# Block-sparse attention and a feed-forward layer on one core: the first pair's operands built by engines, other early transfers and conversions re-ordered

## The chip, the core and the metric

The kernel runs on one core of one Trainium2 chip. The metric is the device time of one execution in microseconds; the time before is the median of three runs, 979.95 us (977.11 to 985.35). PE is the matmul engine, DVE, ACT and POOL are the vector, scalar and GpSimd engines, SP is the engine that issues most transfers.

## What is computed

The reference, cut to what matters:

```python
def _attn_ref(q, k, v, sampled_blocks):            # 4 x 8 heads, S = 768, D = 64, blocks of 32
    scores = np.matmul(q, k.transpose(0, 1, 3, 2)) / np.sqrt(D)
    mask = np.abs(blk_i - blk_j) <= 1              # neighbours, first and last block, sampled blocks
    ...
    scores = np.where(mask, scores, -1000000000.0)
    attn = np.exp(scores - np.max(scores, axis=-1, keepdims=True))
    attn = attn / (np.sum(attn, axis=-1, keepdims=True) + 1e-09)
    return np.matmul(attn, v)

def _moe_ref(x, w_in, w_out):                      # 3072 tokens, 512 -> 2048 -> 512
    h = x @ w_in
    return (h - np.tanh(h)) @ w_out
```

The weights arrive as double precision words; the kernel reads them as pairs of 32-bit words and puts the bits of a single precision number together.

## The kernel before

Thirty-two heads are worked as 16 pairs, then the feed-forward layer follows (`FFN`, units of 512 tokens by 128 hidden columns, 24 + 24 matmuls of 512 columns each). Products are made exact enough by splitting an operand into a high part, which the matmul holds exactly, and a low part, the rest.

A **slot** (`slots`, three of them) holds a pair's operands in four areas: `sA` and `sB` hold the high parts of k and q in partitions 0 to 63, in 64 to 87 the mask by blocks of keys and the one-hot code of the query's block, and in 88 a row of ones and the row of negated maxima; `sC` and `sD` hold the parts for the two cross products. For each pair, `load` fetches k, q and v (SP); `prep_qk` transposes k and q on PE (L198), ACT copies out the high part (`hik`, `hiq`, L200), DVE subtracts for the low part (`lok`, `loq`, L201); `dist` sends 64 partitions at a time into the slot, twelve transfers a pair on SP (L213). `fill` (L185) sends the one-hot code and the mask into each slot, and `setup` makes the mask on DVE (L163 to L178) from two small loads. POOL writes ones to 25 partitions of each slot (L177) and makes the identity.

For each head, `smax` (L255, tiles `sm`) multiplies the high parts for the six query tiles and DVE takes each row's maximum (L259); `smax_fin` transposes the six columns (L264), negates them (`nm`, L266) and sends them to the slot (L267). `qk_exp` (L283, L284, tiles `st`) then forms the full scores with the maximum in, and ACT takes the exponential (`pe`, L287). `split` makes a half precision high and low part (`ph` on ACT or DVE, `pl` on POOL or DVE, L295 to L299), `accum` multiplies them with v (L313 to L322), `norm` divides (L331 to L335), `spill` stores to memory (L341). `prep_v` scales v by its largest magnitude, which starts with a reduction on DVE (`am`, L221).

PSUM holds three `big` tiles (for `sm`, `st`, `pt` and others) and two `one` tiles (for `av`, `pmt`, `pa`).

The first six blocks of weights (`NPRE`) are converted in the attention stage: `load_pre` fetches one (512 KB), `convert_pre` has DVE do three operations of 128 x 512 (L436, L439, L442) and stores the result, and `fetch_w` and `split_w` bring it into a freed slot at the end of attention. Two further blocks are fetched to `stage` by `stage_w`. In the feed-forward stage the same three operations keep their intermediate words in a PSUM tile (`self.cv`).

The order of the work comes from a table of times: each step is put down with `at(time, ...)` in units of one score tile (six to a head, twelve to a pair; head h's maxima run from 6h + TSM on, its exponentials from 6h on), the steps are sorted and called in that order, and a scheduler that simulates the engines then settles each engine's order. Dependencies without a wait (`add_manual_dep` with NoSync) tell it that one instruction shall stand behind another. `urgent` and `after` use them to put later transfers behind the first pair's.

Of the kernel before, what the change touches and what calls it, by code (L numbers as in the profile page):

```python
# [106 lines left out]
def attention(ctx, tc, q, k, v, samp, w_in, w_out, blocks, xscr, ident, ps, slots, wt, f2, ffn):  # L107
# [33 lines left out]
    def load(pr, which="kqv", first=None):  # L141
        r = loads.setdefault(pr, [])
        for nm, src in ((n, x) for n, x in (("k", k), ("q", q), ("v", v)) if n in which):
            t = p2.tile([P, S], F32, tag="raw" + nm, name=f"raw{nm}{pr}", bufs=2)
            d = nc.sync.dma_start(out=t, in_=src[pr])
# [4 lines left out]
    load(0, "kq")  # L150

    def setup():
        for i in range(NV):
# [4 lines left out]
        nc.sync.dma_start(out=sp_i[R, :], in_=samp)
# [4 lines left out]
        nc.vector.tensor_copy(out=sp_f[R, :], in_=sp_i[R, :].rearrange("p (j w) -> p j w", w=2)[:, :, 0])  # L163
        allow = st_sb[R, 0:NB]
        for j in range(3):
            nc.vector.scalar_tensor_tensor(
                out=allow, in0=st_sb[R, NB : 2 * NB], scalar=sp_f[R, j : j + 1], in1=allow, op0=ALU.is_equal, op1=ALU.max
            )
        neg = acst.tile([P, NB], F32, name="neg")
        nc.vector.tensor_scalar(out=neg[R, :], in0=allow, scalar1=1.0, scalar2=-MASKED, op0=ALU.subtract, op1=ALU.mult)  # L170
        nat = p2.tile([P, S], F32, tag="pe", name="nat", bufs=4)
        mk = p2.tile([P, S], F32, tag="pe", name="mk", bufs=4)
        nc.vector.tensor_copy(
            out=nat[R, :].rearrange("p (n j) -> p n j", j=BLK), in_=neg[R, :].unsqueeze(2).to_broadcast([NB, NB, BLK])
        )
        for i in range(NSLOT):
            nc.gpsimd.memset(sA[i].bitcast(F32)[64:89], 1.0)  # L177
        nc.vector.tensor_copy(  # L178
            out=mk[R, :].rearrange("p (t c) -> p t c", t=T), in_=nat[R, :].rearrange("p (c t) -> p t c", t=T)
        )  # L180
        return oh, mk

    def fill(i, dst, src, first=None):
        R = slice(64, 88)
        d = nc.sync.dma_start(out=dst[i].bitcast(F32)[R], in_=src[R, :].unsqueeze(1).to_broadcast([NB, 2, S]))  # L185
# [499 lines left out]
```

## Time and profile before

| | us |
|---|---|
| median of three runs | 979.95 |
| lowest and highest | 977.11, 985.35 |
| profiled execution, its own time | 984.97 |
| its span, first to last instruction | 983.2 |
| PE busy in the span | 922.6 |
| DVE, ACT, POOL busy | 733.4, 629.7, 458.3 |
| mean granted PE clock | 0.977 |

A row of a timeline or of the chain of waits begins with the start in us from the span's start and the duration. A row of the groups ends with the busy time in all, the mean of one in ns, and the idle time of the engine just before, with what ended it. SPq is SP issuing a transfer. A stretch's row gives the busy time of PE, weight loads, DVE, ACT and POOL with their counts, then the granted clock (1.00 also where nothing is recorded), the DMA share and GB/s.

### The profile page before, as it was taken

What the parts mean: (1) busy time and instruction counts of PE and PEld (TensorE: products, weight loads), DVE (VectorE), ACT (ScalarE), POOL (GpSimd) and SP (SyncE); (2) the same over time, 40 slices, a digit from 0 to 9 for tenths busy, and PEclk for the clock granted to TensorE, in tenths of its full rate; (3) what the DMA queues carried; (4) which work ended last, traced back from release to release, by engine and by line L of the source; (5) the groups of instructions that cost most, each with busy time, mean ns of one, the idle gap of its engine ahead of it and who ended that gap; (6) DMA issues with size and microseconds to landing.
All of it is one profiled execution on the core that took longest, in us unless ns stands there. A gap on an engine that the chain in (4) does not pass through costs nothing.

```text
span 983.2 us, 18548 instructions
## 1 busy us (share of the span) xinstructions
PE 922.6 (94%) x7264; PEld 771.1 (78%) x7264; DVE 733.4 (75%) x1119; ACT 629.7 (64%) x943; POOL 458.3 (47%) x308
## 2 busy tenths in 40 slices
PE   5788999999999999888999999999999999999997
PEld 3577788887888878767788888888888888888885
DVE  4589888887887878859999876765676666566664
ACT  1476888888888878656666665555555465555553
POOL 1365877777777777754445422222222222222221
PEclk9698999999999999898999999999999999999999
DMA  8796777676676667114451220210020000001001
GB/s 231 185 274 190 195 175 175 162 174 162 168 173 162 162 161 189 45 48 157 148 168 50 65 76 11 97 33 12 1 75 1 1 33 11 1 1 44 1 1 43
DMA packets 56263, 99.78 MB, mean 101 GB/s; under 512 B 6008, under 2 KB 26680, under 8 KB 56176
## 3 DMA queue, kind: packets, MB, share of 16 engines
q1 hardware_dynamic: 56176, 98.60, 37.0%
q8 instruction: 57, 0.93, 0.4%
q14 instruction: 30, 0.25, 0.1%
HBM read 44.64 MB, written 15.20 MB: 61 GB/s over the span
## 4 chain that ended last, share of the span: by engine, by line
PE 77%; ACT 6%; DMA 5%; DVE 5%; issue 3%; SPq 1%; POOL 1%; ACTq 0%; POOLq 0%; DVEq 0%
PE pf L537 25%; PE pf L569 8%; PE pf L570 8%; PE pf L571 8%; PE st L283 6%; PE st L284 5%; PE sm L255 5%; ACT pe L287 3%; PE av L313 2%; PE av L321 2%; PE av L322 2%; DMA slot<-lok 2%; DMA slot<-nm 2%; DVE mc L259 1%; PE pf L451 1%
## 5 line engine op out<-in xcount | busy, mean ns | idle before, releaser
L299 POOL TENSOR_TENSOR pl<-pe,ph 128x768 f16<-128x768 f32 x173 | 290.0, 1692 | 130.5 <-ACT ph L297 67.5
L560 POOL TENSOR_TENSOR gl<-t,gh 128x512 fp32r<-128x512 f32 x96 | 124.0, 1292 | 358.4 <-ACT gh L559 307.0
L259 DVE TENSOR_REDUCE mc<-sm 128x1 f32<-128x768 f32 x192 | 181.0, 951 | 53.1 <-PE sm L255 49.2
L287 ACT ACTIVATE pe<-st 128x768 f32<-128x768 f32 x192 | 154.1, 805 | 78.4 <-PE st L284 68.5
L283 PE MATMUL st<-slot 128*128 128x512 f32 (+1 forms) x384 | 146.4, 382 | 17.1 <-ACT pe L287 13.4
L552 DVE TENSOR_TENSOR t<-t,pf 128x512 f32<-128x512 f32 x94 | 64.5, 686 | 123.3 <-ACT t L546 123.2
L559 ACT ACTIVATE gh<-t 128x512 fp32r<-128x512 f32 x96 | 60.6, 632 | 120.2 <-DVE t L556 120.2
L297 ACT ACTIVATE ph<-pe 128x768 f16<-128x768 f32 x154 | 130.0, 844 | 4.7
L284 PE MATMUL st<-slot 89*128 89x512 f32 (+1 forms) x384 | 126.1, 349 | 1.0 <-DMA slot<-nm 1.0
L313 PE MATMUL av<-vhl,ph 128*128 128x65 f16 x1152 | 120.7, 195 | 0.0
L322 PE MATMUL av<-vhl,pl 128*128 128x65 f16 x1152 | 119.6, 194 | 0.9 <-POOL pl L299 0.9
L255 PE MATMUL sm<-slot 88*128 88x512 f32 (+1 forms) x384 | 111.1, 376 | 9.6 <-DMA slot<-hiq 7.0
L321 PE MATMUL av<-vhl,ph 128*128 128x64 f16 x1152 | 119.7, 196 | 0.0
L313 PEld LDWEIGHTS <-ph 128*128 128x128 f16 x1152 | 106.6, 97 | 13.6 <-issue 12.9
L322 PEld LDWEIGHTS <-pl 128*128 128x128 f16 x1152 | 107.9, 100 | 3.0 <-issue 1.5
L321 PEld LDWEIGHTS <-ph 128*128 128x128 f16 x1152 | 107.9, 98 | 0.7 <-issue 0.5
L544 ACT ACTIVATE u<-pf 128x512 f32<-128x512 f32 x94 | 56.2, 598 | 80.5 <-PE pf L537 80.2
L283 PEld LDWEIGHTS st<-slot 128*128 128x128 f32 x384 | 74.9, 195 | 35.1 <-ACT pe L287 18.5
L284 PEld LDWEIGHTS st<-slot 89*128 89x128 f32 x384 | 75.5, 197 | 11.2 <-DMA slot<-nm 2.2
L255 PEld LDWEIGHTS sm<-slot 88*128 88x128 f32 x384 | 62.6, 202 | 17.0 <-DMA slot<-mk 6.3
L570 PE MATMUL pf<-wx,gh 128*128 128x512 f32 x192 | 74.7, 389 | 0.0
L569 PE MATMUL pf<-wx,gh 128*128 128x512 f32 x192 | 74.7, 389 | 0.0
(123 smaller groups left out, 1962.8 us busy)
## 6 DMA issues: line engine op xcount, KB each, us to landing
slot<-hik SPq DMA_DIRECT2D x64, 192.0 KB
slot<-hiq SPq DMA_DIRECT2D x64, 192.0 KB
stage<-w_in SPq DMA_DIRECT2D x13, 512.0 KB
stage<-w_out SPq DMA_DIRECT2D x13, 512.0 KB
rawk<-k SPq DMA_DIRECT2D x16, 384.0 KB
rawq<-q SPq DMA_DIRECT2D x16, 384.0 KB
slot<-lok SPq DMA_DIRECT2D x32, 192.0 KB
slot<-loq SPq DMA_DIRECT2D x32, 192.0 KB
```

What stands on the lines that cost most here:

```text
L255: nc.tensor.matmul(pm[:, c], lhsT=sB[s][0:88, j, t * P : (t + 1) * P], rhs=sA[s][0:88, j, c], start=True, stop=True)
L259: maxed.append(nc.vector.tensor_reduce(out=mcs[h][:, t : t + 1], in_=pm[:, 0:S], op=ALU.max, axis=AX.X))
L283: ms.append(nc.tensor.matmul(st[:, c], lhsT=sC[s][:, j, kc], rhs=sD[s][:, j, c], start=True, stop=False))
L284: ms.append(nc.tensor.matmul(st[:, c], lhsT=sA[s][0:89, j, kc], rhs=sB[s][0:89, j, c], start=False, stop=True))
L287: nc.scalar.activation(out=pe, in_=st[:, 0:S], func=AF.Exp, scale=0.125)
L299: d = eng.tensor_tensor(out=pl, in0=pe, in1=ph, op=ALU.subtract)
L313: m = nc.tensor.matmul(o[:, t, :], lhsT=ph[:, c], rhs=vv[:, 0:65], start=(kt == 0 and t == 0), stop=False, skip_group_check=True)
L321: nc.tensor.matmul(o[:, t, 0:64], lhsT=ph[:, c], rhs=vv[:, 65:129], start=False, stop=False, skip_group_check=True)
L322: m = nc.tensor.matmul(o[:, t, :], lhsT=pl[:, c], rhs=vv[:, 0:65], start=False, stop=last, skip_group_check=True)
L537: nc.tensor.matmul(h, lhsT=w[:, cc], rhs=x[:, c, :], start=(k == 0), stop=(k == 3 * NCT - 1))
L569: nc.tensor.matmul(o, lhsT=gh[:, c], rhs=wo[0][ft], start=(ft == f0), stop=False)
L570: nc.tensor.matmul(o, lhsT=gh[:, c], rhs=wo[1][ft], start=False, stop=False)
```

## The change

*The first pair.* Pair 0 has no `prep_qk` and no `dist` any more. Two further inputs, `k0` and `q0`, hold its two heads laid out with 64 rows of 768 tokens. Eight loads of 64 x 768 bring each of them to both halves of a tile (`twice`). ACT, POOL and DVE write the high and low parts straight into slot 0, and DVE and POOL write the mask and the one-hot code there too. The three small loads of `setup` go out on ACT's queue; the slots' mask areas 1 and 2 are copied from slot 0.

*Order of early transfers.* The next pair's k and q, v of pair 0 and the fills stand behind the eight loads; k of pair 1 and so on behind the negated maxima of the first two heads. The two `stage_w` loads, before free to go first, stand behind the latest `nm` transfer at time 170 (`late`).

*Conversions.* `load_pre` stands behind the latest `nm` transfer, the first operation of a conversion behind the latest maximum and the latest negation (`behind`), ten units after its load and not four, and its intermediate words go to a `one` tile of PSUM. `prep_v`'s reduction stands behind both as well.

*Token order.* Token s of a head lies in tile s // 128, partition s % 128 (before: tile s % 6, partition s // 6), in inputs, mask and output rows; sizes and counts of these transfers are as before.

The core of the diff:

```diff
-W0, DW = 40, 24.7
+W0, DW = 40, 24
-TV0 = -4
+TV0 = -1
+ST0 = 170
...
+    M = slice(64, 88)
+    twice = [[p2.tile([P, S], F32, tag="pe", name=f"twice{nm}{j}", bufs=4) for nm in "kq"] for j in range(2)]
+    def load_first():
+        for j in range(2):
+            for half in range(2):
+                for src, dst in zip((k0, q0), twice[j]):
+                    urgent[0].append(nc.sync.dma_start(out=dst[64 * half : 64 * half + 64, :], in_=src[j]))
+    def first_high(j):
+        for x, dst in enumerate((sA, sB)):
+            nc.scalar.activation(out=dst[0][0:64, j], in_=twice[j][x][0:64], func=AF.Copy)
+    def first_low(j):
+        kk, qq = twice[j]
+        nc.scalar.activation(out=sC[0][64:128, j], in_=kk[64:128], func=AF.Copy)
+        nc.scalar.activation(out=sD[0][0:64, j], in_=qq[0:64], func=AF.Copy)
+        nc.gpsimd.tensor_tensor(out=sC[0][0:64, j], in0=kk[0:64], in1=sA[0].bitcast(F32)[0:64, j], op=ALU.subtract)
+        nc.vector.tensor_tensor(out=sD[0][64:128, j], in0=qq[64:128], in1=sB[0].bitcast(F32)[0:64, j], op=ALU.subtract)
...
-        nc.sync.dma_start(out=sp_i[R, :], in_=samp)
-        nc.sync.dma_start(out=st_sb[R, :], in_=blocks)
+        nc.scalar.dma_start(out=sp_i[M, :], in_=samp)
+        nc.scalar.dma_start(out=st_sb[M, :], in_=blocks[:, 0 : 2 * NB])
+        nc.scalar.dma_start(out=oh[M, :], in_=blocks[:, 2 * NB :])
...
+        for j, eng in enumerate((nc.vector, nc.gpsimd)):
+            eng.tensor_copy(out=sB[0][M, j], in_=oh[M, :])
+            eng.tensor_copy(
+                out=sA[0][M, j].rearrange("p (n c) -> p n c", c=BLK), in_=neg[M, :].unsqueeze(2).to_broadcast([NB, NB, BLK])
+            )
...
-    def fill(i, dst, src, first=None):
+    def fill(i):
+        after(0, nc.sync.dma_start(out=sB[i].bitcast(F32)[M], in_=oh[M, :].unsqueeze(1).to_broadcast([NB, 2, S])))
+        after(0, nc.sync.dma_start(out=sA[i].bitcast(F32)[M], in_=sA[0].bitcast(F32)[M]))
...
+    def behind(d):
+        for f in maxed[-1:] + negated[-1:]:
+            tc.add_manual_dep(
+                d.ins, f.ins.name, mybir.DependencyInfo(mybir.DependencyClass.NoSync, mybir.DependencyReason.DATA), reason="late"
+            )
+    def late(d):
+        tc.add_manual_dep(
+            d.ins, moved[-1].ins.name, mybir.DependencyInfo(mybir.DependencyClass.NoSync, mybir.DependencyReason.DATA), reason="late"
+        )
...
-        for nm, dt in (("k", 0), ("q", 0.5)):
+        for nm, dt in (("k", 0), ("q", 0.5)) if pr else ():
...
-        d = load_w(nc, wraw[m, ft], w_in, w_out, m, ft)
-        if ft == 0:
-            after(2, d)
+        late(load_w(nc, wraw[m, ft], w_in, w_out, m, ft))
-        nc.sync.dma_start(out=wt[m, ft], in_=convert(nc, f2, wraw[m, ft], f"cvt{m}{ft}"))
+        nc.sync.dma_start(out=wt[m, ft], in_=convert(nc, f2, wraw[m, ft], f"cvt{m}{ft}", one(f"cv{m}{ft}"), behind))
-        at(W0 + DW * x + 4, convert_pre, "io"[x % 2], x // 2)
+        at(W0 + DW * x + 10, convert_pre, "io"[x % 2], x // 2)
-        at(F0 + 1, ffn.stage_w, i)
+        at(ST0, lambda i: late(ffn.stage_w(i)), i)
...
-                nc.sync.dma_start(out=self.out[b * S : (b + 1) * S, :].rearrange("(p t) d -> t p d", t=T)[t], in_=ob)
+                nc.sync.dma_start(out=self.out[(b * T + t) * P : (b * T + t + 1) * P, :], in_=ob)
```

What this does to the engines' orders shows at three places. The first is SP's queue up to the first head's negated maxima (`nm`). Before, ahead of these rows stand the loads of pair 0, the two small ones, the two stage loads, two fills and the first four slot transfers:

```order
L145 DMA rawk_159<-k 128x768
L145 DMA rawq_161<-q 128x768
L213 DMA slot_73<-hik_132 64x768 x2
L213 DMA slot_73<-lok_133 64x768 x2
L213 DMA slot_73<-hiq_146 64x768 x2
L213 DMA slot_73<-loq_147 64x768 x2
L145 DMA rawv_171<-v 128x768
L185 DMA slot_74<-st_sb 24x2x768
L185 DMA slot_74<-mk 24x2x768
L185 DMA slot_75<-st_sb 24x2x768
L185 DMA slot_75<-mk 24x2x768
L267 DMA slot_73<-nm_204 1x6x128
```

Now, with six loads like the first two rows ahead of them and nothing else:

```order
L154 DMA twicek_102<-k 64x768
L154 DMA twiceq_103<-q 64x768
L142 DMA rawk_143<-k 128x768
L142 DMA rawq_145<-q 128x768
L142 DMA rawv_147<-v 128x768
L200 DMA slot_68<-oh 24x2x768
L200 DMA slot_69<-oh 24x2x768
L201 DMA slot_68<-slot_67 24x1536
L201 DMA slot_69<-slot_67 24x1536
L291 DMA slot_67<-nm_190 1x6x128
```

The slot transfers of pair 0 and the stage loads are gone from ahead of `nm`; the four fills still stand just before it. The second place is DVE's queue where the first conversion stands. Before, it comes with the second one in the work on the first two pairs, between reductions (L259), the low parts of a pair (L201) and v's scale (`sb`):

```order
L335 TENSOR_TENSOR xq_551<-av_360,rs_552 128x6x64
L436 TENSOR_SCALAR cvti_1900<-rawi_1744 128x512
L232 TENSOR_REDUCE sb_498<-pa_496 128x1
L439 SCALAR_TENSOR_TENSOR cvti_1900<-rawi_1744,cvti_1900 128x512
L436 TENSOR_SCALAR cvto_2863<-rawo_2706 128x512
L295 CAST ph_4_668<-pe_4_565 128x768
L235 TENSOR_SCALAR sb_498<-sb_498 128x1
L442 SCALAR_TENSOR_TENSOR cvti_1900<-rawi_1744,cvti_1900 128x512
L201 TENSOR_TENSOR lok_572<-ptk_573,hik_571 128x768
L439 SCALAR_TENSOR_TENSOR cvto_2863<-rawo_2706,cvto_2863 128x512
```

Now it stands alone, behind head 9's negation, and the normalisation of head 7 (L356 to L360) is mixed with it:

```order
L290 TENSOR_SCALAR nm_2087<-pmt_2085 6x128
L283 TENSOR_REDUCE mc_2143<-sm_1_2159 128x1
L460 TENSOR_SCALAR cvi_2130<-rawi_1730 128x512
L356 SCALAR_TENSOR_TENSOR rs_2203<-av_2022,sb_1352 128x6
L465 SCALAR_TENSOR_TENSOR cvi_2130<-rawi_1730,cvi_2130 128x512
L359 RECIPROCAL rs_2203<-rs_2203 128x6
L283 TENSOR_REDUCE mc_2143<-sm_2_2215 128x1
L468 SCALAR_TENSOR_TENSOR cvti_2131<-rawi_1730,cvi_2130 128x512
L360 TENSOR_TENSOR xq_1966<-av_2022,rs_2203 128x6x64
```

The conversion moved from pairs 0 and 1 to pair 4, its words now lie in `cvi`, a PSUM tile, and the other five follow at distances of two pairs. The third place is SP's queue at the end of attention, behind head 29's `nm`, where the slots' room is fetched full of converted weights (`wi`, `wo`). Before:

```order
L267 DMA slot_75<-nm_6839 1x6x128
L341 DMA xscr_63<-xq_6709 768x1x128
L494 DMA slot_75<-wo_77 128x512
L494 DMA slot_75<-wi_80 128x512
L494 DMA slot_75<-wo_79 128x512
L494 DMA slot_75<-wi_76 128x512
L267 DMA slot_73<-nm_7068 1x6x128
```

And now:

```order
L291 DMA slot_69<-nm_6825 1x6x128
L448 DMA stage_83<-w_in 128x4x256
L452 DMA stage_84<-w_out 128x1024
L520 DMA slot_69<-wi_74 128x512
L520 DMA slot_69<-wo_71 128x512
L407 DMA wo_75<-cvto_6865 128x512
L366 DMA xscr_63<-xq_6700 768x1x128
L520 DMA slot_69<-wo_73 128x512
L520 DMA slot_69<-wi_70 128x512
L291 DMA slot_67<-nm_7062 1x6x128
```

The two stage loads and the store of the last conversion came in between head 29's and head 30's `nm`, ahead of or among the fetches. On PE, the twelve transposes of pair 0 at the very start are gone; its order from there to the end of attention changes in places only.

More of the change, by code (lines that the diff above doesn't have):

```diff
@@ L75, in attention_ffn @@
 @with_exitstack
-def attention_ffn(ctx, tc, q, k, v, samp, w_in, w_out, blocks, out):
+def attention_ffn(ctx, tc, q, k, v, k0, q0, samp, w_in, w_out, blocks, out):
     nc = tc.nc
@@ L130, in in_order @@
         chain.append(last)
-    urgent = [[], [], []]
+    urgent = [[], []]
     def after(n, d):
@@ L164, in setup @@
[L164 to L172, printed above, removed]
@@ L213, in dist @@
                 d = nc.sync.dma_start(out=dst[s].bitcast(F32)[r0 : r0 + 64, j], in_=src.bitcast(F32)[64 * j : 64 * j + 64])
-                if pr == 0:
-                    urgent[part].append(d)
+                if pr == 1:
+                    after(1, d)
     def prep_v(pr):
-        rv = loads[pr][2]
+        rv = loads[pr]["v"]
         vf = rv.rearrange("p (n d) -> p n d", d=D)
@@ L223, in prep_v @@
         )
-        if pr > 1:
-            tc.add_manual_dep(
-                d.ins, maxed[-1].ins.name, mybir.DependencyInfo(mybir.DependencyClass.NoSync, mybir.DependencyReason.DATA), reason="late"
-            )
+        behind(d)
         pa = one(f"pa{pr}")
@@ L351, in at @@
         ev.append((time, len(ev), f, args))
-    at(-17.0, fill, 0, sB, onehot)
-    at(TQK + 0.3, fill, 0, sA, mask, 0)
-    at(TQK + 0.9, load, 1, "kq", 0)
-    at(TQK + 1.7, load, 0, "v", 1)
+    for j in range(2):
+        at(TSM - 0.5 + 3 * j, first_high, j)
+        at(TSM + 1 + 3 * j, first_low, j)
+    at(TSM - 0.2, load, 1, "kq", 0)
+    at(TSM - 0.1, load, 0, "v", 0)
     for i in range(1, NSLOT):
-        for dst, src in ((sB, onehot), (sA, mask)):
-            at(TQK + TF * i, fill, i, dst, src, 1)
+        at(TSM + TF * i, fill, i)
     for pr in range(NPAIR):
@@ L661, in pairs @@
     def pairs(a, *order):
-        return np.asarray(a).reshape(NPAIR, 2, P, T, D).transpose(order).reshape(NPAIR, P, S)
+        return np.asarray(a).reshape(NPAIR, 2, T, P, D).transpose(order).reshape(NPAIR, P, S)
     arrays = {
-        "q": pairs(inputs["q"], 0, 2, 3, 1, 4),
-        "k": pairs(inputs["k"], 0, 2, 3, 1, 4),
-        "v": pairs(inputs["v"], 0, 2, 1, 3, 4),
+        "q": pairs(inputs["q"], 0, 3, 2, 1, 4),
+        "k": pairs(inputs["k"], 0, 3, 2, 1, 4),
+        "v": pairs(inputs["v"], 0, 3, 1, 2, 4),
+        "k0": np.asarray(inputs["k"])[0, :2].transpose(0, 2, 1),
+        "q0": np.asarray(inputs["q"])[0, :2].transpose(0, 2, 1),
         "samp": words(inputs["sampled_blocks"]),
```

77 lines of the change are left out of this document (37 added, 40 removed).

## The prediction

> **What bounds the kernel now.** I read the page's head first, then the busy time by stretches, cut where a head pair's first exponential starts: pair 0 at 33.5 us, pair 1 at 65.1, pair 2 at 97.0, pair 3 at 119.8, pair 4 at 143.3.
>
> ```profile
> span 983.2 us, 18548 instructions
> 0.00:14.20 14.20, 2.82 (x13) 2.46 (x13) 4.61 (x14) 2.90 (x3) 4.71 (x9) 1.00 0.80 229
> 14.20:33.50 19.30, 12.44 (x38) 8.93 (x39) 11.00 (x15) 1.66 (x3) 0.00 (x0) 0.82 0.98 222
> 33.50:65.10 31.60, 28.51 (x297) 23.68 (x297) 24.27 (x36) 22.47 (x28) 19.22 (x11) 0.84 0.78 216
> 65.10:97.00 31.90, 26.97 (x305) 22.42 (x305) 28.58 (x43) 19.82 (x26) 20.57 (x11) 0.89 0.76 220
> 97.00:119.80 22.80, 21.00 (x249) 17.58 (x249) 20.24 (x32) 19.58 (x26) 18.72 (x11) 1.00 0.68 193
> 119.80:143.30 23.50, 22.58 (x305) 19.57 (x305) 19.54 (x30) 19.79 (x26) 18.01 (x11) 1.00 0.71 175
> 447.00:983.20 536.20, 528.79 (x2357) 435.64 (x2355) 382.27 (x583) 303.84 (x528) 155.51 (x121) 0.99 0.14 45
> ```
>
> The columns are the stretch, its length, busy PE, weight loads, DVE, ACT, POOL, then granted clock, DMA share and GB/s. From 447 us on PE is busy 99% of the time: the feed-forward stage is bound by matmuls, and the change leaves its matmuls alone. A settled pair (119.8 to 143.3) takes 23.5 us with PE busy 22.58, so PE bounds it too, while DVE has 3.96 us to spare. What stands out is the beginning. Until 33.5 us no exponential runs, and DMA is 80% and then 98% busy. Pairs 0 and 1 then take 31.6 and 31.9 us, some 8 us each above the settled pair. So 33.5 us of start and 16.5 us of slow pairs are on offer; the rest hardly is. Next, the chain of waits and the timeline of the start.
>
> ```profile
> 1.03 3.99 POOL slot L177 x3
> 13.69 8.72 DMA slot<-lok
> 22.47 0.82 SPq L185
> 25.10 7.05 DMA slot<-nm
> 33.46 0.82 ACT pe L287
> ```
>
> ```profile
> 0.75 0.39 SPq L145 DMA_DIRECT2D rawk<-k  x1
> 1.66 0.44 SPq L158 DMA_DIRECT2D sp_i<-samp  x1
> 4.96 0.16 DVE L163 CAST sp_f<-sp_i 24x3 f32<-24x3 int32 x1 [3.87 <-DMA sp_i<-samp]
> 7.02 0.81 ACT L200 ACTIVATE hik<-ptk 128x768 fp32r<-128x768 f32 x1 [4.99 <-PE ptk L198]
> 7.20 0.85 DVE L178 COPY mk<-nat 24x768 f32<-24x768 f32 x1
> 14.20 6.50 PE L255 MATMUL sm<-slot 88*128 88x512 f32 x16 [5.94 <-DMA slot<-hiq]
> 22.14 0.27 DVE L266 TENSOR_SCALAR nm<-pmt 6x128 fp32r<-6x128 f32 x1
> ```
>
> The first score matmul for the maxima (sm) starts at 14.20, on a transfer of hiq into the slot. Head 0's maxima are ready on DVE at 22.14, but their transfer (nm) is issued at 25.10, after SP's four fills, and lands 7.05 us later, at 32.15, because the queues are full. The exponential follows 1.31 us after that.
>
> **The change, part by part.** *The start.*
>
> ```profile
> slot<-hik SPq DMA_DIRECT2D x64, 192.0 KB
> rawk<-k SPq DMA_DIRECT2D x16, 384.0 KB
> stage<-w_in SPq DMA_DIRECT2D x13, 512.0 KB
> L299 POOL TENSOR_TENSOR pl<-pe,ph 128x768 f16<-128x768 f32 x173 | 290.0, 1692 | 130.5 <-ACT ph L297 67.5 <-issue 21.1 <-PE av L322 20.8
> ```
>
> Removed for pair 0: twelve transposes, twelve slot transfers (12 x 192 = 2304 KB), the two loads of 384 KB, two fills, and ahead of them the two stage loads of 512 KB, which move to the end of attention. Added: eight loads of 64 x 768 (8 x 192 = 1536 KB) and engine copies straight into the slot. Before nm, SP now issues 1536 + 3 x 384 + four fills of 24 x 1536 words (144 KB each) = 3264 KB, some 3.34 MB. At the 222 to 229 GB/s of the first two rows that is 15 us of transfers from about 2 us on, done at 17.
>
> When can sm start? The small load samp was issued behind rawk and rawq (768 KB) and its reader ran at 4.96, so the first 768 KB had landed by then at the latest: the four twice loads of head 0 are as many bytes. ACT needs 0.81 us for the high part of k and 0.81 for q: 6.6. The mask chain took from 4.96 to 8.05 (7.20 plus 0.85) with both its copies; its loads now go out on ACT's queue, not behind the operands, and its two big writes go straight into the slot. I put sm at 6.5, with 5.7 (loads a little earlier) and 7.5 (mask as late as now) as ends.
>
> From sm to head 0's nm took 22.14 - 14.20 = 7.94 us, paced by DVE's reductions. DVE now also subtracts q's low part of head 1 in between, L165. No row of this form exists; between 0.85 (the copy above) and 1.69 (POOL's subtraction L299) I take 0.95. The low parts of head 0, the copies L162 and L163 and POOL's L164 run beside the maxima and are read only by st. So nm is ready at 15.4, SP has no fill left and issues at 15.6. Its landing lies between 3.30 (samp, 1.66 to 4.96, also behind loads) and 7.05; the queue is nearly drained, so I take 3.3: 18.9, and the exponential at 20.2 against 33.46: **-13.3 us**. The ends: 5.7 and 3.3 give 19.4 (-14.1); 7.5, a full 1.69 and 7.05 give 26.6 (-6.9). Covered at no cost: ACT's three load issues and its table load run while the operands travel, and SP's eight issues, at rawk's 0.39 us each 3.1 us in all, end at 3.9, before the operands they bring can have landed; without that cover they would cost those 3.1 us.
>
> *Conversions out of pairs 0 and 1.*
>
> ```profile
> L439 DVE SCALAR_TENSOR_TENSOR cvti<-rawi,cvti 128x512 int32<-128x512 int32 x3 | 3.9, 1307 | 0.0
> L436 DVE TENSOR_SCALAR cvti<-rawi 128x512 int32<-128x512 int32 x3 | 1.3, 418 | 2.6 <-DMA rawi<-w_in 2.6
> L439 DVE SCALAR_TENSOR_TENSOR pf<-stage,pf 128x512 int32<-128x512 int32 x26 | 17.9, 690 | 0.1
> L436 DVE TENSOR_SCALAR pf<-stage 128x512 int32<-128x512 int32 x26 | 17.9, 688 | 0.1
> L442 DVE SCALAR_TENSOR_TENSOR cvti<-stage,pf 128x512 int32<-128x512 int32 x13 | 8.8, 678 | 0.1
> 26.70:43.80 17.10, 12.52 (x65) 9.43 (x66) 10.13 (x14) 7.21 (x9) 6.37 (x4) 0.50 0.69 157
> 81.30:88.20 6.90, 6.81 (x37) 6.05 (x38) 6.14 (x12) 3.92 (x5) 4.16 (x3) 0.51 0.35 116
> ```
>
> All six early weight conversions now lie in pairs 0 and 1 (the first rows: two at the end of pair 0, four in pair 1, where DVE even waits 2.6 us for a load). In pair 1 DVE is busy 28.58 of 31.9 us: it, not PE, sets the pace there. Pair 0 has two causes. Its clock of 0.84 over 31.6 us costs 0.16 x 31.6 = 5.1 us, the remaining 3.0 us go with its conversions. The half clock lasted to 43.8 although PE was busy 12.52 of 17.1 us, so I let pair 0 keep its 5.1 us after an equally broken start, and take **-3.0**; the ends are 0 and -8.1. Pair 1's clock dip of 6.9 us follows a stretch in which DVE held PE up; it should go with the conversions: 31.9 to 23.9, **-8.0** (ends -4.9, dip kept, and -8.4). Pair 2 makes up 0.7 us at 22.80; without arrears it takes 23.5: **+0.7**.
>
> The first row, with both inputs in SBUF, took 1307 ns, the third, with one in PSUM, 690. The Trainium skill, page "SBUF — State Buffer", section "Who interferes with whom", says that a VectorE instruction with two SBUF inputs and a GpSimd instruction that reads SBUF hold that port one after the other, and these rows agree. It speaks against the start: L165 and L164 are such a pair. By that rule the start could be up to 1.7 us later and the forecast 962; no row here shows it at that place.
>
> *The same conversions in the middle.* Each now stands behind a head's nm on DVE, one in two pairs, and costs what the feed-forward conversions cost, whose intermediate words are in PSUM already: 688 + 690 + 678 ns = 2.06 us. A settled pair has 3.96 us of DVE to spare, so most is hidden. But on DVE there stand behind the first operation the previous head's normalisation and the next reductions, for which PE waits with the three big PSUM tiles, and the conversion holds one of the two small ones, which the next head's accumulation needs. Unseen here; ends 0 and 6 x 2.06 = +12.4, I take 0.5 us each, nearer to the slack's zero: **+3**. The load is issued ten tiles (some 20 us) ahead, so the 2.6 us wait for it goes.
>
> *The end of attention.*
>
> ```profile
> 386.51 5.05 DMA slot<-nm
> 393.73 4.39 DMA slot<-wi
> 398.15 0.63 ACT L497 ACTIVATE slot<-slot 128x512 fp32r<-128x512 f32 x1 [1.51 <-DMA slot<-wi]
> 400.00:410.00 10.00, 8.04 (x105) 6.79 (x103) 10.00 (x15) 7.87 (x12) 8.66 (x7) 0.95 0.17 54
> 410.00:420.00 10.00, 10.00 (x125) 8.83 (x124) 6.40 (x12) 5.92 (x8) 6.41 (x4) 0.71 0.01 3
> ```
>
> The two stage loads (1024 KB, 4.7 us at 225 GB/s) now stand on SP ahead of the fetches, and ACT stands at 398.15 waiting for the fetch issued at 393.73, with exponentials queued behind it. The loads go out right after head 29's nm (386.51 in the first row), some 6 us before that fetch's 393.73, so most has passed by then. Ends 0 and +4.7, I take **+1**. Token order, mask order and output rows change only which rows a transfer names; sizes and counts stay: 0.
>
> **Sum:** -13.3 - 3.0 - 8.0 + 0.7 + 3 + 1 = -19.6. The profiled execution took 984.97 us (span 983.2), so its like would take 965.4. It lies 5.0 us above the median of the runs shown, 979.95 (977.11 to 985.35), on which the forecast stands: 979.95 - 19.6 = **960.4 us**.
>
> **Rivals.**
>
> *The clock is granted early.* PE has matmuls from 6.5 us on and the gaps are shorter; if the clock is full before pair 0, its 5.1 us go too: 955. Against it: in the present start PE ran sm back to back from 14.20 and was at half clock again from 26.7. The skill's page "TensorE: Matmul & The Clock Gate", Part 1 ("The HAM clock gate"), says one busy window of about 3.4 us frees the clock, which would make this the likeliest case; the 17.1 us at 0.50 with PE 73% busy speak against taking it so plainly. Chance 0.20.
>
> *The wait moves to the queue.* nm lands as late after its issue as now, or the mask or port holds sm: -6.9 instead of -13.3, 967. For it: DMA is still full until about 17 us; pair 1's twelve transfers (2304 KB, 10 us) follow. Chance 0.17.
>
> *The middle pays in full.* Six conversions at 2.06 us, +12.4 instead of +3: 970. For it: in pair 1 they cost their whole time; against it, DVE had no slack there and it has 3.96 us in a settled pair. Chance 0.12.
>
> *Slower than before: each conversion trips the clock.* If one delays DVE until PE stands idle for its 2.06 us, the clock may fall by half as at 81.3 us, where 6.9 us at 0.51 lost 3.4 us: 5.5 us each, 33 in all, against 22.6 gained (all terms but the middle's): 990. It decides from 22.6 / 6 = 3.8 us per conversion. Against it: by the code's table (TSM) the reductions run about ten tiles ahead of the exponentials that need them. Chance 0.03. That nothing moves (the conversions drift back early, the start stays queue-bound) I give 0.02; the order of the built program speaks against it.
>
> **Numbers.** My forecast has 0.46. The range runs from 948 (start -14.1, clock full, nothing paid later, less the spread of the runs) to 971, which takes in the queue and the full middle and leaves out the slower case. A measurement of this kernel can tell about 1%, 9.8 us, from no change: faster than 970.2 is nearly all of the forecast (0.45), the early clock (0.20), most of the queue's case (0.15) and half of the full middle (0.06), together 0.86; slower 0.03; the rest, 0.11, within.
>
> **What would show it.** Right: the first sm near 6.5 us, the first exponential between 19 and 22, pair 1 near 24 us with DVE under 23, pairs with a conversion at most 24.5, the three operations near 690 ns each, the feed-forward stage 536 us. Wrong: an nm that lands after 24 us, a conversion pair over 26 us or with a clock under 1, or ACT held more than 5 us by the fetched weights.

## The result, and the profile after

| | before | changed |
|---|---|---|
| median of three runs, us | 979.95 (977.11 to 985.35) | 970.86 (970.11 to 971.74) |
| ratio, 95% interval | | 0.9884 [0.9848, 0.9920] |
| profiled execution, its span | 984.97, 983.2 | 970.11, 968.2 |
| mean granted clock | 0.977 | 0.988 |

The change took 9.1 us off the median, where 19.6 were forecast: faster, and 0.1 us inside the upper end of the range, 971. With later runs of the same two kernels (four of the changed one, seven of the one before) it is 972.29 against 983.95, a ratio of 0.9881 [0.9856, 0.9906], 11.7 us; this 972.29 lies outside the range.

First the busy time by stretches, with the columns of the prediction: pair 0, 1 and 2, pairs 3 to 13, pairs 14 and 15, and the rest.

```profile
0.00:21.45 21.45, 11.46 (x38) 8.44 (x39) 18.18 (x28) 9.39 (x12) 11.22 (x13) 1.00 0.68 169
21.45:46.49 25.04, 23.53 (x281) 19.36 (x281) 21.44 (x31) 20.45 (x26) 18.08 (x11) 1.00 0.84 234
46.49:75.69 29.20, 25.78 (x303) 21.68 (x300) 19.15 (x31) 19.64 (x27) 18.21 (x11) 0.88 0.60 149
75.69:98.25 22.56, 21.38 (x268) 18.34 (x267) 20.43 (x32) 19.24 (x26) 17.97 (x11) 1.00 0.70 175
98.25:363.72 265.47, 250.37 (x3346) 216.10 (x3345) 222.00 (x346) 218.47 (x276) 198.19 (x122) 1.00 0.73 181
363.72:411.93 48.21, 42.16 (x575) 36.63 (x573) 39.31 (x55) 35.49 (x48) 35.89 (x23) 0.93 0.42 124
411.93:968.20 556.27, 539.01 (x2458) 443.63 (x2454) 393.92 (x602) 310.44 (x540) 161.12 (x124) 0.99 0.14 47
```

Each stretch begins with the first exponential of its pair. The prediction's own stretches began one exponential late from pair 1 on (65.1 for 63.46, 97.0 for 95.81, 119.8 for 118.78); with the right ones the kernel before had 30.0, 32.35 and 22.97 us in pairs 0 to 2. Term by term, all in the two profiled executions:

| stretch | before | after | difference | forecast |
|---|---|---|---|---|
| start, until the first exponential | 33.46 | 21.45 | -12.0 | -13.3 |
| pair 0 | 30.00 | 25.04 | -5.0 | -3.0 |
| pair 1 | 32.35 | 29.20 | -3.2 | -8.0 |
| pair 2 | 22.97 | 22.56 | -0.4 | +0.7 |
| pairs 3 to 13 (five conversions) | 262.79 | 265.47 | +2.7 | +3, with the sixth |
| pairs 14, 15 and the rest | 601.6 | 604.5 | +2.9 | +1 |
| sum | 983.2 | 968.2 | -15.0 | -19.6 |

The start in the timeline; the brackets hold the wait ahead of an instruction and what ended it:

```profile
5.08 1.80 POOL L164 TENSOR_TENSOR slot<-twicek,slot 64x768 fp32r<-64x768 f32 x1
...
5.23 1.68 DVE L186 TENSOR_SCALAR neg<-st_sb 24x24 f32<-24x24 f32 x1
...
7.49 1.17 DVE L188 CAST slot<-oh 24x768 fp32r<-24x768 f32 x1
...
8.81 0.77 PE L279 MATMUL sm<-slot 88*128 88x512 f32 x1 [8.81 <-DVE slot L188]
...
18.22 0.27 DVE L290 TENSOR_SCALAR nm<-pmt 6x128 fp32r<-6x128 f32 x1
...
18.51 0.70 SPq L291 DMA_DIRECT2D slot<-nm  x1
...
20.73 0.39 PE L309 MATMUL st<-slot 89*128 89x512 f32 x1
...
21.45 0.81 ACT L312 ACTIVATE pe<-st 128x768 f32<-128x768 f32 x1 [0.33 <-DVE sb L243]
```

The first score matmul waits for the mask's last copy on DVE and starts at 8.81. The maxima are negated by 18.49, issued at 18.51, and the matmul that reads them (L309) runs at 20.73 without a wait for them: they landed in at most 2.2 us, where head 0's took 7.05 before.

Then pair 1, which is the largest miss. First its waits (total, times, longest), then the timeline around the gap (DVE, SP, PE), then two stretches in the gap and after it:

```profile
PE st L309 <- DMA slot<-nm: 3.3, 1, 3.3
```

```profile
51.35 0.27 DVE L290 TENSOR_SCALAR nm<-pmt 6x128 fp32r<-6x128 f32 x1
...
51.56 0.61 SPq L366 DMA_DIRECT2D xscr<-xq  x1
...
53.08 0.75 SPq L291 DMA_DIRECT2D slot<-nm  x1
...
58.95 0.80 PE L309 MATMUL st<-slot 89*128 89x512 f32 x1 [3.32 <-DMA slot<-nm]
```

```profile
55.60:58.95 3.35, 0.03 (x2) 0.01 (x1) 0.08 (x1) 0.52 (x1) 2.99 (x2) 0.81 0.53 150
57.70:64.50 6.80, 5.55 (x40) 4.56 (x41) 1.34 (x2) 2.93 (x4) 2.54 (x2) 0.50 0.03 8
```

Head 3's maxima are ready at 51.62, issued at 53.08 behind pair 2's operands (from 40.1 to 53 us SP issued two loads of k and q, v, twelve slot transfers and a store, 3840 KB), and only at 58.95 does PE go on. PE stands 3.32 us, and for 6.80 us, from 57.70 and so still within the gap, it has half its clock. DVE is busy 19.15 of the pair's 29.20 us: no conversion is in it any more.

The conversions, by groups, and the end of attention (SP's fetch in the chain of waits, and PE's gap in the timeline):

```profile
L465 DVE SCALAR_TENSOR_TENSOR cvi<-rawi,cvi 128x512 int32<-128x512 int32 x3 | 2.1, 696 | 0.0
...
L460 DVE TENSOR_SCALAR cvi<-rawi 128x512 int32<-128x512 int32 x3 | 2.1, 685 | 0.0
...
L468 DVE SCALAR_TENSOR_TENSOR cvti<-rawi,cvi 128x512 int32<-128x512 int32 x3 | 2.0, 679 | 0.0
```

```profile
376.02 5.35 DMA slot<-wi
```

```profile
382.77 0.80 PE L308 MATMUL st<-slot 128*128 128x512 f32 x1 [3.01 <-ACT pe L312]
```

The three operations take 696, 685 and 679 ns as forecast. At the end a fetch took 5.35 us (4.39 before), ACT stood for it with exponentials behind, PE stood 3.01 us (2.06 before), and the clock fell there, in pair 14, for 6.8 us (before, for as long in pair 15).

### The profile page after: what moved, and what is told of

Read it like the earlier page. It is cut to its first block, busy times and chain, and to the rows that moved or that the text cites. A ratio compares the mean times of both kernels' runs of the same rounds, so it can differ in the third digit from the quotient of the medians.

```text
span 968.2 us, 18528 instructions
## 1 busy us (share of the span) xinstructions
PE 913.7 (94%) x7252; PEld 764.2 (79%) x7252; DVE 734.4 (76%) x1119; ACT 633.1 (65%) x949; POOL 460.7 (48%) x312
## 4 chain that ended last, share of the span: by engine, by line
PE 77%; DVE 9%; ACT 5%; issue 4%; DMA 4%; SPq 0%; ACTq 0%; DVEq 0%; POOL 0%; POOLq 0%
PE pf L563 26%; PE pf L595 8%; PE pf L596 8%; PE pf L597 8%; PE st L308 6%; PE sm L279 5%; PE st L309 5%; PE av L338 3%; ACT pe L312 3%; PE av L346 3%; PE av L347 2%; DVE mc L283 2%; DMA slot<-nm 2%; PE pf L477 1%; DMA rawk<-k 1%
## 5 line engine op out<-in xcount | busy, mean ns | idle before, releaser
L324 POOL TENSOR_TENSOR pl<-pe,ph 128x768 f16<-128x768 f32 x173 | 285.6, 1668 | 108.8 <-ACT ph L322 41.9
L308 PE MATMUL st<-slot 128*128 128x512 f32 (+1 forms) x384 | 144.0, 376 | 15.1 <-ACT pe L312 14.1
L309 PE MATMUL st<-slot 89*128 89x512 f32 (+1 forms) x384 | 124.4, 345 | 3.7 <-DMA slot<-nm 3.7
L309 PEld LDWEIGHTS st<-slot 89*128 89x128 f32 x384 | 74.5, 194 | 13.3 <-DMA slot<-nm 4.6
L582 DVE COPY_PREDICATED t<-mk,pf 128x512 f32<-128x512 int32 x94 | 70.0, 744 | 6.9 <-DVE pf L581 0.5
L596 PE MATMUL pf<-wx,gh 128*128 128x512 f32 x192 | 74.8, 390 | 0.0
```

Source lines behind the costliest of these rows:

```text
L308: ms.append(nc.tensor.matmul(st[:, c], lhsT=sC[s][:, j, kc], rhs=sD[s][:, j, c], start=True, stop=False))
L309: ms.append(nc.tensor.matmul(st[:, c], lhsT=sA[s][0:89, j, kc], rhs=sB[s][0:89, j, c], start=False, stop=True))
L324: d = eng.tensor_tensor(out=pl, in0=pe, in1=ph, op=ALU.subtract)
L596: nc.tensor.matmul(o, lhsT=gh[:, c], rhs=wo[1][ft], start=False, stop=False)
```

## The experiments

Two theories were set against each other. **D**: pair 1 was long because DVE had the conversions in it. **Q**: it is long because a head's negated maxima reach the slot late, behind bulk transfers on SP's queue, and the conversions only stood beside that.

**1. The conversions' move alone, on the kernel before.** `behind` and `late`, as in the change, and the two lists that they use are left out here.

```diff
-W0, DW = 40, 24.7
+W0, DW = 40, 24
-        d = load_w(nc, wraw[m, ft], w_in, w_out, m, ft)
-        if ft == 0:
-            after(2, d)
+        late(load_w(nc, wraw[m, ft], w_in, w_out, m, ft))
-        nc.sync.dma_start(out=wt[m, ft], in_=convert(nc, f2, wraw[m, ft], f"cvt{m}{ft}"))
+        nc.sync.dma_start(out=wt[m, ft], in_=convert(nc, f2, wraw[m, ft], f"cvt{m}{ft}", one(f"cv{m}{ft}"), behind))
-        at(W0 + DW * x + 4, convert_pre, "io"[x % 2], x // 2)
+        at(W0 + DW * x + 10, convert_pre, "io"[x % 2], x // 2)
```

> The kernel before with the change's treatment of the six conversions alone: load behind the latest maxima transfer, ten units ahead, first operation behind the latest maximum and negation, intermediate words in PSUM, one in two pairs. Start, pair 0's operands and stage loads as before. Theory D (pair 1's old excess over a settled pair was the conversions' DVE time): pair 1 falls from 32.4 us to about 24, pair 0 by 1 to 3, the middle gains some 3.5 us as in the changed kernel: 5 to 8 us less than before. Theory Q (pair 1 is long because head 3's negated maxima reach the slot late through a full queue, conversions or not): pair 1 stays at 29 us or more, and the kernel is within 3 us of before, on either side.

Measured: 984.43 us against 981.56, ratio 1.0022 [0.9994, 1.0050]. Pairs 0, 1, 2:

```profile
31.52:59.32 27.80, 26.95 (x272) 22.40 (x271) 20.10 (x31) 20.88 (x27) 18.71 (x11) 0.80 0.71 191
59.32:87.54 28.22, 24.95 (x309) 21.09 (x308) 19.05 (x31) 20.15 (x26) 18.08 (x11) 0.94 0.61 143
87.54:114.40 26.86, 23.34 (x269) 19.46 (x268) 20.63 (x33) 19.92 (x26) 18.58 (x11) 0.94 0.66 160
```

And what PE waited for in these three pairs:

```profile
PE st L296 <- DMA slot<-nm: 4.1, 2, 2.5
```

DVE fell from 29.03 to 19.05 us in pair 1, but the pair only from 32.35 to 28.22, and pair 2 rose by 3.9: two late maxima take part of the conversions' place. Pair 1 lies between the 24 us that D expected and the 29 of Q. The three pairs together gain 2.4 us, and pairs 3 to 13 took 2.4 us more. D alone falls: moving the conversions is worth nothing measurable while the old start is there.

**2. The changed kernel with the conversions early again**, words in SBUF (the lines of the diff above, the other way round, with `after(1, d)`).

> The changed kernel with the six conversions where they were before (loads behind the first two heads' maxima, four units ahead, no tie, words in SBUF); the new start, the other early transfers and the late stage loads stay. Pair 4, 6, 8, 10, 12 should fall back by 0.4 to 1.0 us each, 3.3 us in all, whatever the theory. Theory D: pairs 0 to 2 take 8 us more again, so 975 us or so. Theory Q: the conversions' 3 MB of loads and 1.5 MB of stores come back into the same queue and the DVE operations run partly in PE's waits: pairs 0 to 2 take 3 to 8 us more, 971 to 976 us. If it is under 968, moving the conversions brought nothing.

Measured: 977.34 us, ratio 0.9950 [0.9930, 0.9970] to before: 6.5 us slower than the changed kernel's 970.86, and above what either theory expected. Pair 1 and one operation's group:

```profile
48.68:85.67 36.99, 29.16 (x304) 23.35 (x300) 31.25 (x46) 20.05 (x25) 19.85 (x11) 0.86 0.81 219
```

```profile
L470 DVE SCALAR_TENSOR_TENSOR cvti<-rawi,cvti 128x512 int32<-128x512 int32 x3 | 5.1, 1696 | 0.0
```

With the new start pair 1 takes 37.0 us when the conversions are in it: DVE is busy 31.25 us, and the same operation that took 679 ns now takes 1696, with its words in SBUF again. So D is a part: the conversions do cost there, but two causes lie in one pair, and taking away one leaves the other. All of the change but the conversions is worth 4.2 us (977.34 against 981.56), the conversions' new treatment, place and words in PSUM together, 6.5 on top of that and nothing without it. Early conversions with their words in PSUM were not run; experiments 8 and 9 say more on the words.

**3. Head 3's maxima ahead of pair 2's operands for the cross products.** In `dist` the eight transfers to `sC` and `sD` are kept in a list, and in `smax_fin`, where `d` is the transfer of `nm`, they are put behind it:

```diff
+                if pr == 2 and part == 1:
+                    held.append(d)
...
+        if h == 3:
+            for x in held:
+                tc.add_manual_dep(
+                    x.ins, d.ins.name, mybir.DependencyInfo(mybir.DependencyClass.NoSync, mybir.DependencyReason.DATA), reason="held"
+                )
```

> The changed kernel with eight transfers of pair 2 (the operands of the cross products, 8 x 192 KB) put behind the transfer of head 3's negated maxima on SP's queue; nothing else. Theory Q: that transfer lands in 2 to 3 us and not in 5.8, PE's gap of 3.3 us at 55.6 us and the 6.8 us at half clock after it go, pair 1 takes 23.5 to 24.5 and not 29.2, and the kernel 965 to 966 us. Rival: what is moved is late next, pair 2's scores wait for it and pair 2 gains what pair 1 loses: 970 us. Rival of the clock: the gap shrinks but the clock falls all the same: 967 to 968.

Measured: 966.73 us (962.98 to 967.24), 4.1 under the changed kernel; each of the four runs lies under every run of it. SP's queue and pair 1:

```profile
53.08 0.76 SPq L294 DMA_DIRECT2D slot<-nm  x1
53.90 1.15 SPq L227 DMA_DIRECT2D slot<-hik  x2
```

```profile
46.55:70.58 24.03, 23.20 (x303) 19.76 (x300) 18.87 (x31) 19.67 (x27) 18.11 (x11) 1.00 0.77 190
```

The maxima are issued at the same 53.08, but PE has no wait for them any more, the clock stays at 1.00, and pair 1 takes 24.03 us: within 0.2 of the 23.9 that the prediction gave it. Pair 2 takes 22.9 (22.6), so what was put back is not late there. Q is shown for the changed kernel's pair 1, to 5.2 of the 5.3 us by which it missed its forecast length.

**4. POOL's subtraction away from the mask's making.** `copied` holds POOL's last copy of the mask.

```diff
-        nc.gpsimd.tensor_tensor(out=sC[0][0:64, j], in0=kk[0:64], in1=sA[0].bitcast(F32)[0:64, j], op=ALU.subtract)
+        d = nc.gpsimd.tensor_tensor(out=sC[0][0:64, j], in0=kk[0:64], in1=sA[0].bitcast(F32)[0:64, j], op=ALU.subtract)
+        tc.add_manual_dep(
+            d.ins, copied[-1].ins.name, mybir.DependencyInfo(mybir.DependencyClass.NoSync, mybir.DependencyReason.DATA), reason="port"
+        )
```

> The changed kernel with POOL's subtraction of k's low part (first head) put behind POOL's own two copies of mask and code; nothing else. The DVE operation that makes the mask's 24 x 24 values took 1.68 us in the changed kernel, from 5.23 to 6.91, while POOL's subtraction ran from 5.08 to 6.88. If DVE was held by POOL there (a shared port): it takes under 0.3 us, the first score matmul starts at 7.2 to 7.6 and not at 8.81, and the kernel loses 1.2 to 1.6 us, if the maxima's transfer does not give it back. If the operation is that slow by itself: nothing changes, 970 to 971 us.

Measured: 970.82 us, no faster than the changed kernel. DVE, POOL and PE at the start:

```profile
5.26 0.17 DVE L190 TENSOR_SCALAR neg<-st_sb 24x24 f32<-24x24 f32 x1
...
7.33 0.98 PE L284 MATMUL sm<-slot 88*128 88x512 f32 x2 [7.33 <-POOL ident masks.py:199]
...
8.93 3.60 POOL L164 TENSOR_TENSOR slot<-twicek,slot 64x768 fp32r<-64x768 f32 x2
...
11.06 2.28 DVE L168 TENSOR_TENSOR slot<-twiceq,slot 64x768 fp32r<-64x768 f32 x1
```

The same 24 x 24 operation takes 0.17 us and not 1.68, and the first score matmul starts at 7.33: DVE had been held by POOL. But POOL's two subtractions now run from 8.93 to 12.53, and DVE's second subtraction, 0.95 us before, takes 2.28 beside them. The wait only moved. The Trainium skill, page "SBUF — State Buffer", section "Who interferes with whom", says that a VectorE instruction with two SBUF inputs contends with a GpSimd instruction that reads SBUF, and that copies, casts and tensor_scalar operations of VectorE can take the shared port too; both rows (2.28 and 1.68 us) agree.

**5. Both subtractions off the way.** As in 4, and DVE's subtraction for the second head behind the first head's negation (`if j: behind(d)`), with the second head's step later in the table of times (`TSM + 1 + 5 * j` for `3 * j`).

> The kernel of the port experiment, and DVE's subtraction of q's low part of the second head put behind the first head's negated maxima. There, the mask operation fell from 1.68 to 0.17 us and the first score matmul started at 7.33, but the second subtraction on DVE then took 2.28 us beside POOL's second one and PE stood 2.38 us for the reductions. Port theory: with no DVE subtraction among the reductions the maxima are ready at 15.7 us and not at 18.0 (18.5 in the changed kernel), the first exponential starts near 19.0 (21.45), and the kernel takes 967.5 to 969. Rival (queue): the transfer of the maxima is issued earlier but lands no earlier, because the loads ahead of it are not through before 17 to 18 us; first exponential 20 to 21 us, kernel 970 to 971.

Measured: 971.01 us (969.31 to 972.10). The maxima are ready at 15.43, the first exponential starts at 19.44, 2.0 us earlier, and the kernel is no faster. DVE and SP around head 3's maxima, and pair 1:

```profile
49.57 0.27 DVE L297 TENSOR_SCALAR nm<-pmt 6x128 fp32r<-6x128 f32 x1
...
50.61 0.61 SPq L373 DMA_DIRECT2D xscr<-xq  x1
53.20 0.76 SPq L298 DMA_DIRECT2D slot<-nm  x1
```

```profile
44.20:73.85 29.65, 25.02 (x303) 20.97 (x300) 18.87 (x31) 19.75 (x26) 18.19 (x11) 0.94 0.63 147
```

The maxima are ready 1.8 us earlier (49.84 for 51.62) and are issued at the same time, behind the store of the first pair; PE's gap grows to 4.2 us. Pair 1 and pair 3 (26.9 us for 25.0) take the 2 us back. So the start came as the port theory forecast, and the kernel's time as the rival did, but for another reason than the rival's.

**6. The stage loads behind the last head's maxima** (`ST0 = 184` for 170).

> The changed kernel with the two stage loads (1 MB) put behind the last head's maxima transfer instead of head 29's; nothing else. In the changed kernel ACT stands 2.86 us for the fetch that is queued behind them, PE stands 3.0 us at 379.8 and the clock falls for 6.8 us: 6.4 us. Theory Q: the fetch lands earlier, the gap shrinks to the 2.06 us of the kernel before or less and the clock stays: pairs 14 and 15 take 43 to 45 us and not 48.2, and the kernel 966 to 968. Rival: the fetch waits for its own 5 us of landing anyway, as before the change (46.5 us for both pairs with a gap of 2.06 and a fall of the clock later): 969 to 971.

Measured: 971.07 us (967.38 to 975.71), no difference. Pairs 14 and 15:

```profile
369.84:416.09 46.25, 41.38 (x575) 35.66 (x573) 39.96 (x55) 35.63 (x48) 35.86 (x23) 0.96 0.46 128
```

2.0 us less there, 1.4 us more in the rest of the profiled execution (557.7 for 556.3). Both theories hold in part: with the loads out of the way the fetch takes 3.94 us and not 5.35, ACT stands 0.97 us for it and not 2.86, and PE 1.62 and not 3.01; but it is still waited for, and the clock still falls, for 3.4 us. What the loads ahead of it cost is too small to show in the kernel's time.

**7. The stage loads ahead of the first maxima** (`at(F0 + 1, ffn.stage_w, i)` as before the change).

> The changed kernel with the two stage loads free to go early, as before the change: in the built order they stand just ahead of the first head's maxima transfer. By the sums: 1024 KB at 225 GB/s, so that transfer lands 4.7 us later and the first exponential starts near 26 us and not at 21.45. PE then stands some 5 us. Theory C (a gap of PE of some 3 us or more takes the full clock away for two windows or more, as at 23.8 us in the kernel before): pair 0 runs in part at half clock and takes 28 to 31 us and not 25.0, while the end gains 1 to 4 us: 974 to 980. If the clock stays: 971 to 975. If the loads hide: 968 to 971.

Measured: 973.35 us (968.59 to 974.04), ratio 0.9902 [0.9873, 0.9931] to before, not clear of the changed kernel's 0.9884. PE at the first scores:

```profile
21.99 0.50 PE L309 MATMUL st<-slot 89*128 89x512 f32 x1 [1.09 <-DMA slot<-nm]
```

1 MB ahead cost 1.26 us (21.99 for 20.73), not 4.7: DMA, 70% busy from 8.8 to 18.5 us in the changed kernel, was full in that stretch instead. That price, which the prediction had used at the end of attention, was a rate applied where the queue had room. Yet pair 1 grew to 31.0 us; that bytes which went out early are missing later would explain it, but is not shown. Pair 0 took 25.6 us with 3.4 us at half clock, so theory C was not put to its test: the gap was too small.

**8. The late conversions with their words in SBUF** (`None` for `one(f"cv{m}{ft}")`).

> The changed kernel with the intermediate words of the six late conversions in SBUF, as before the change, so that they hold no PSUM tile; nothing else. From the rows of before (418 and 1307 ns, two of the latter) a conversion takes 3.0 us of DVE and not 2.06. If DVE's time decides in a pair with a conversion, each costs up to 1 us more: 971 to 977. If the held PSUM tile decides (the next head's accumulation waits for it), each costs 0.4 to 0.7 us less: 967 to 969. If the slack hides both: within 1 us of 970.9.

Measured: 980.57 us (974.73 to 984.97 in ten runs), 9.7 us slower, above every range expected, ratio 0.9993 [0.9969, 1.0018] to before: without PSUM the change brings nothing. The groups, and one operation on DVE with POOL's rows beside it:

```profile
L468 DVE SCALAR_TENSOR_TENSOR cvto<-rawo,cvto 128x512 int32<-128x512 int32 x3 | 6.1, 2030 | 0.0
...
L465 DVE SCALAR_TENSOR_TENSOR cvti<-rawi,cvti 128x512 int32<-128x512 int32 x3 | 4.0, 1347 | 0.0
...
L460 DVE TENSOR_SCALAR cvto<-rawo 128x512 int32<-128x512 int32 x3 | 1.4, 476 | 0.0
```

```profile
127.08 3.71 POOL L324 TENSOR_TENSOR pl<-pe,ph 128x768 f16<-128x768 f32 x2 [0.22 <-ACT ph L322]
...
129.32 2.03 DVE L468 SCALAR_TENSOR_TENSOR cvti<-rawi,cvti 128x512 int32<-128x512 int32 x1
```

The last operation waits for POOL's subtraction to end (130.79) and then does its 0.6 us; with one input in PSUM the changed kernel's operations take 0.68 to 0.70, and the first two of pair 4 run beside POOL's subtractions (128.59 to 131.85). A conversion takes 3.8 us of DVE in the mean (849 or 476, 1347 or 1322, 1582 or 2030 ns), and pairs 3 to 13 take 271.94 for 265.47 us in the profiled execution. That execution was the fastest of the ten; where the others lost up to 10 us more is not shown.

**9. Words in PSUM without the tie** (loads and times as in 2, `one(...)` kept, `behind` gone).

> The changed kernel with the six conversions' words in PSUM, but loads (first two heads' maxima ahead, four units before the conversion) and operations free as before, with no tie to maxima. In the built order they do not go back to pairs 0 and 1: the PSUM tile that each takes in turn keeps them in the middle, the first near the place that it has in the changed kernel. If the words in PSUM are what counts (the kernel with words in SBUF took 980.57): 970 to 972. If the tie behind maximum and negation counts as much: 975 or more. Only the loads of the first two go out early, 1 MB in the full queue of pairs 0 to 2, worth up to 4.7 us.

Measured: 971.46 us (970.68 to 975.36). The first conversion ends at 120.7, the others about 48 us apart, so the PSUM tile that each takes in its turn keeps them in the middle, and the tie to the maxima brings nothing that can be measured.

**10. Experiments 3 and 5 together, and the first store behind head 3's maxima** (`if pr == 0: late(d)` in `spill`).

> The changed kernel with both subtractions off the start (first exponential at 19.44 in that experiment), pair 2's eight cross-product transfers behind head 3's maxima transfer, and the first store behind it too (it was issued at 53.2 where the maxima were ready at 49.84). Theory Q: the 2 us that the start alone gained and pair 1 took back stay now; pair 0 24.8, pair 1 23.5 to 24.5, no gap over 1.5 us before 100 us: 963 to 965, some 2 us under the 966.73 of the reordering alone. If the full queue still takes it back: 966 to 967.

**11. The same with the stage loads of 6**, and **12, the changed kernel again.**

> The kernel of the experiment beside it with the two stage loads behind the last head's maxima transfer as well. Alone that shrank the gap at the end of attention from 3.0 to 1.6 us and pairs 14 and 15 from 48.2 to 46.2, and the stage after it took 1.4 us more. If the two cancel: the same as the kernel beside it within 1 us. If the 2 us are to be had: 961 to 963.

> The changed kernel once more, as the measure for the kernels beside it on the same chip: 970 to 972, with pair 1 at 29 to 32 us.

Measured on one chip: 963.39 us (960.96 to 964.13), 960.36 (958.14 to 966.65) and 972.29 (970.31 to 974.19), with 983.95 for the kernel before; ratios to it 0.9786 [0.9763, 0.9810], 0.9770 [0.9731, 0.9809] and 0.9881. Pairs 0, 1 and 2 of the eleventh:

```profile
20.26:45.01 24.75, 23.17 (x281) 19.20 (x281) 20.57 (x32) 20.70 (x27) 18.70 (x11) 1.00 0.83 223
45.01:68.20 23.19, 23.08 (x303) 19.70 (x300) 19.10 (x31) 19.57 (x27) 18.12 (x11) 1.00 0.78 185
68.20:91.39 23.19, 21.50 (x268) 18.34 (x267) 20.40 (x32) 19.25 (x27) 17.91 (x11) 1.00 0.69 171
```

PE is busy 23.08 of 23.19 us in pair 1, with a clock of 1.00, and pair 2 ends 2.1 us earlier than in experiment 3 (91.39 for 93.47; 92.32 in the tenth): the start's gain stays once the queue does not take it back. Both kernels beat the change, by 9 and 12 us on that chip. Between the two of them the runs overlap, and pairs 14 and 15 take 46.9 and 46.4 us, so what the stage loads add is not shown. The twelfth lies 0.3 us over what was expected of it, with pair 1 at 28.4 us.

## Why the prediction was right, and where it was short

**Sign, bound and place: right.** PE sets the pace, the feed-forward stage kept its 539 us of PE work, and the gain lies wholly in the start and in pairs 0 and 1: 20.2 us in the profiled executions.

**Start, -12.0 for -13.3: near, by errors that partly cancel.** The score matmul came at 8.81, 2.3 us after the forecast and after the late end of 7.5. The term took the mask's making as the rows of before had it; the new code ran POOL's subtraction beside it, which held DVE for 1.5 us (experiment 4); the prediction had seen the port for L165 and L164, not for the mask. From the score matmul to the maxima it took 9.7 us, 0.8 more than the sum has. Against that, the transfer was priced at 3.3 us and took at most 2.2, and the exponential came 0.7 us after L309 and not 1.31. The prediction's late end is also added up wrongly: its terms, 7.5 + 7.94 + 1.69 + 0.2 + 7.05 + 1.31, give 25.7 and not 26.6, so its rival of the queue would be 966 and not 967.

**Pair 0, -5.0 for -3.0: the first rival happened.** The records hold the full clock from 20.1 to 57.7 us, so pair 0 did not keep its 5.1 us. The start has no gap of 6 us any more, as before at 23.8. The rule that the prediction took from the Trainium skill, page "TensorE: Matmul & The Clock Gate", Part 1 ("The HAM clock gate"), that one busy window of about 3.4 us frees the clock, spoke for this case. The trace agrees in the result; the first record of the full clock, though, comes 11.3 us after the first matmul, across one gap of 1.05 us. With 5.1 us gone for the clock nothing would be left for the 3.0 that the prediction gave the conversions. Experiments 1 and 2 put these at some 2 us (27.80 for 30.00, and 26.83 against 25.04), which leaves some 3 for the clock, an estimate: the split was off too. No experiment changed the clock alone.

**Pair 1, -3.2 for -8.0: the step that failed.** The prediction put all 8 us to the conversions ("it should go with the conversions: 31.9 to 23.9"). They went, and the queue took their place: 3.3 us of gap and the clock's fall after it. The rival "the wait moves to the queue" was priced for head 0 only. Pair 1's waits in the kernel before could not tell it, since no wait of PE for nm stood there; the longest in total was one for DVE's maxima:

```profile
PE st L283 <- DVE mc L259: 2.2, 3, 1.0
```

But the sum never asked what would be late next: 3840 KB are issued ahead of head 3's maxima between 40 and 53 us. Experiment 3 puts it right: pair 1 at 24.03.

**Middle, +2.7 for +3: right in size, but too small to be shown.** The pairs with one of the first five conversions take 1.0, 0.8, 0.5, 0.4 and 0.6 us more than in the kernel before, 0.66 each for 0.5. But single executions differ by as much. Pairs 3 to 13 in experiment 2, which has no conversion there, and in the eleventh, which has five:

```profile
109.72:374.18 264.46, 249.99 (x3346) 215.48 (x3345) 214.48 (x331) 218.78 (x276) 198.14 (x121) 1.00 0.69 165
91.39:355.73 264.34, 249.99 (x3346) 215.99 (x3345) 221.91 (x346) 218.66 (x276) 198.28 (x122) 1.00 0.74 183
```

Pairs 4 and 6 take 24.66 and 24.48 us in experiment 2, as long as in the changed kernel (24.52, 24.44). So the full price of 2.06 us each did not come; whether a conversion there costs half a microsecond or nothing stays open. What the prediction did not see is what this rests on. It took the words in PSUM for a matter of 690 for 1307 ns; experiment 8 shows that without them the whole gain goes.

**End, +2.9 for +1: too small, with the cause shown only in part.** The fetch landed 1 us later, as priced, PE's gap grew by 1 us to 3.0, and the clock fell in pair 14 (29.93 us). But before, it fell for as long in pair 15; pairs 14 and 15 of the kernel before:

```profile
381.57:407.75 26.18, 23.45 (x306) 19.69 (x304) 22.16 (x34) 21.22 (x30) 21.32 (x14) 1.00 0.57 156
407.75:428.07 20.32, 18.88 (x266) 17.03 (x267) 14.73 (x19) 14.08 (x19) 14.86 (x10) 0.83 0.08 22
```

Pair 15 now takes 18.28 us, so the two together grew by 1.8. The other 1.1 us lie in the feed-forward stage; what made them was not followed.

**The last step, from the profiled execution to the median.** The sum missed by 4.7 us on its own time (970.11 for 965.4), but by 10.5 on the median. The profiled execution lay 5.0 us above the median of three; other runs of the kernel before had medians of 981.56, 981.97 and 983.95 (19, 13 and 7 runs, 977.3 to 987.1 in all). The changed kernel's executions all lie between 970.1 and 974.2. So the median of three on which the forecast stood lay 1.6 to 4 us low, and that the result fell inside the range, by 0.1 us, is luck as much as a right sum: against the last of these medians the gain is 11.7 us, still far from 19.6. The 5 us cannot be carried over whole: part of what an execution loses more than another seems to lie in the stretches that the change shortens. That is argued, not shown.

## What to carry to other kernels

When a stall goes, write down what is issued ahead of the next small transfer that PE needs; a 3 KB transfer behind 3840 KB cost 5.2 us, and moving eight issues behind it won them back. Put one input of a two-input DVE operation, and the words that it writes in between, into PSUM where POOL works beside it: here, with the conversions in the same pairs, that was the difference between 980.57 and 970.86 us, of which the traces show 6.5 in pairs 3 to 13. A gain at the start that does not pass the next full queue is no gain, so test the pieces together as well as apart.

## What the hardware showed

A 24 x 24 operation on DVE took 1.68 us beside POOL's subtraction and 0.17 without it. In these traces most gaps of PE of 1.6 us or more in attention are followed by 3.4 or 6.8 us at half clock (3.32 by 6.8, 3.01 by 6.8, 1.64 in experiment 1 by 3.4; not so 2.71 in experiment 5), while those of about 0.95 us, one in each settled pair, have none. So a wait of 3.3 us cost pair 1 5.2 us. And 1 MB ahead of a small transfer delayed it by 1.26 us where DMA had been 70% busy.
